# Exponentials of attention: some tiles by a polynomial on VectorE and GpSimd, the wide activations in parts

## The chip, the cores and the metric

The kernel runs on one core of a Trainium2 chip. The metric is the device time of one execution in microseconds (us), as the median of several runs. A NeuronCore has five engines, each with its own queue of instructions, which they work off in order: TensorE (PE in the profile; its weight loads are PEld), VectorE (DVE), ScalarE (ACT), GpSimd (POOL) and SyncE (SP, which here only issues transfers). They share a memory SBUF of 128 partitions; TensorE writes into PSUM, from where VectorE and ScalarE read. Engines wait for each other by semaphores.

## The reference

The network has four layers on x of 2048 positions and 640 channels: a state-space convolution, attention, the same convolution, the same attention, each behind a layer norm and added to x. The change lies in the attention, which runs twice (layers b and d in the kernel's names):

```python
x = x + _A_ref(_layernorm(x), ...)          # long convolution
x = x + _B_ref(_layernorm(x), ...)          # attention
...
q = (x @ wq).reshape(B, S, H, Dh)           # S = 2048, H = 32 heads, Dh = 20
k = x @ wk                                  # one key and one value
v = x @ wv                                  # for all heads
scores = einsum("bhqd,bkd->bhqk", q, k) * (Dh ** -0.5)
p = softmax(scores, axis=-1)
o = einsum("bhqk,bkd->bhqd", p, v)
... reshape(B, S, H * Dh) @ wo
```

Per attention layer this is 32 x 2048 x 2048, or 134 million, exponentials.

## The kernel before

One layer's scores are cut into 1024 tiles of 128 keys by 1024 columns; the columns are four heads by 256 queries. The list `tiles` runs over four blocks of 512 queries (`nb`), eight groups of four heads (`hg`), two halves of the block (`f`) and sixteen key tiles (`t`). 32 consecutive tiles belong to one head group and add up into one PSUM tile `po`.

A tile goes through three steps. `scores` (L1298) makes two matmuls into a PSUM tile `sc` of 1024 columns. The exponential is taken in one of two ways. `direct` (L1304): ScalarE reads `sc` and writes the exponentials to an SBUF tile `pt`. `aside` (L1311): VectorE copies `sc` to one half of a wide SBUF tile `pw`, and ScalarE later takes the exponentials of the 2048 columns of two such tiles in place, with one activation (L1429). `values` (L1321) multiplies the exponentials by the values, four matmuls of 256 columns, one for each head, into `po`. The value matrix has a column of ones, so that the sum of the exponentials, the softmax's denominator, comes with it.

PSUM has room for three tiles `sc` (tag `s2`, three buffers taken in turn), and two smaller banks, one for `po`, the other for the projections of the head group before. `qp`, the queries of a head group, comes by 16 transfers issued on SyncE, with three buffers; `load_q` is called when the first tile of a group is scored.

Within the loop the order of instructions on TensorE, ScalarE and VectorE is the order in which the code is written (`manual_schedule`). The loop takes six tiles per cycle: four direct, two aside. The cycle starts with the wide activation, and then has two halves. A half issues three scores, each followed by its exponential or copy (direct, aside, direct, in the order of the three PSUM buffers), then one step of a waiting list `pieces`, and then `behind`: the values of three earlier tiles, and, where a credit of 0.52 per half has reached 1, one projection (`product`, L1393) with the addition to x that follows it on VectorE (`add`, L1380).

When a head group's 32 tiles are through, `normalize` copies `po` out of PSUM (L1347) and transposes it at once; the reciprocal with a second transposition and the multiplication by it (L1352) are the two `pieces` of the next halves. The last one also issues the transfers of the result to `ot` on SyncE (L1358), from which the projections read.

Of the kernel before, what the change touches and what calls it, by code (L numbers as in the profile page):

```python
# [36 lines left out]
LIMIT = 32.0 * 20.0**0.5  # L37
SAFE = ((LIMIT - 1e-6) / 1.002) ** 2


# [155 lines left out]
class Net:  # L196
    def __init__(self, tc, ins):
        self.tc = tc
        self.nc = tc.nc
        self.ins = ins  # L200
        self.wfs = []
        self.bank = 0

    def setup(self, ctx):
# [16 lines left out]

    def ps2(self, name):
        return self.ps.tile([P, 1024], F32, tag="s2", bufs=3, name=name)

# [1037 lines left out]
    def main_loop(self, ap, mp, kt, vt, nm, out):  # L1262
# [24 lines left out]
        tiles = [(nb, hg, f, t) for nb in range(4) for hg in range(8) for f in range(2) for t in range(16)]  # L1287
        pos, pts, ots, wide = {}, {}, {}, {}
        queue, later = [], []

        def scores(i):
            nb, hg, f, t = tiles[i]
            if (nb, hg) not in qps:
                self.load_q(ap, nm, nb, hg)
            sc = self.ps2(f"sc{nm}{i}")
            for par in range(2):
                rows = slice(64 * par, 64 * par + 62)
                nc.tensor.matmul(sc[:, 512 * par : 512 * par + 512], kt[rows, 128 * t : 128 * t + 128],  # L1298
                                 qps[nb, hg][rows, f].rearrange("p a c -> p (a c)"), start=True, stop=True)
            return sc  # L1300

        def direct(i, sc):
            pts[i] = mp.tile([P, 1024], F32, tag="pt", bufs=5, name=f"pt{i}")
            nc.scalar.activation(pts[i], sc, AF.Exp, scale=SCALE)  # L1304

        def aside(i, sc):

            if i // 6 not in wide:
                wide[i // 6] = mp.tile([P, 2, 1024], F32, tag="pw", bufs=3, name=f"pw{i // 6}")
            pts[i] = wide[i // 6][:, i % 6]  # L1310
            nc.vector.tensor_copy(pts[i], sc)  # L1311

        def values(i):
            nb, hg, f, t = tiles[i]
            if (nb, hg) not in pos:
                pos[nb, hg] = self.ps1(f"po{nm}{nb}{hg}", hg % 2)
            po, pt = pos[nb, hg], pts.pop(i)

            for j in range(4):
                c0 = 512 * (j % 2) + 256 * (j // 2)  # L1320
                nc.tensor.matmul(po[32 * j : 32 * j + 32, 256 * f : 256 * f + 256], vt[:, t],  # L1321
                                 pt[:, c0 : c0 + 256], start=(t == 0), stop=(t == 15))

# [17 lines left out]
        def flat(a):  # L1341
            return a.rearrange("p a b -> p (a b)")

        def normalize(nb, hg):
            po = pos.pop((nb, hg))
            on = mp.tile([P, 512], F32, tag="on", bufs=2, name=f"on{nb}{hg}")
            nc.vector.tensor_copy(on, po)  # L1347
            inv, steps = inverses(on, f"{nb}{hg}")
            steps[0]()

            def finish():
# [8 lines left out]
                for k in range(80 * hg // 128, 80 * (hg + 1) // 128):  # L1360
                    later.extend((nb, k, u) for u in range(8))

            pieces.extend([steps[1], finish])

# [37 lines left out]

        n = len(tiles)
        credit, pieces = [0.0], []

        def behind(group):

            for i in group:
                values(i)
                if i % 32 == 31 and i + 1 < n:  # L1410
                    normalize(*tiles[i][:2])
            if not group:
                return
            if group[-1] % 32 >= (15 if group[-1] < n - 32 else 8):
                queue.extend(later)
                later.clear()
            credit[0] = min(credit[0] + 0.52, 1.5)
            if queue and credit[0] >= 1 and group[-1] % 32 not in (0, 1):
                credit[0] -= 1
                projection(tiles[group[-1]][1])  # L1420

        with tc.manual_schedule(engines={mybir.EngineType.PE, mybir.EngineType.Activation,
                                         mybir.EngineType.DVE}):
            for i, put in ((0, direct), (6, aside), (1, direct)):
                put(i, scores(i))
            for c in range(0, n, 6):
                w = wide.pop(c // 6, None)
                if w is not None:
                    nc.scalar.activation(flat(w), flat(w), AF.Exp, scale=SCALE)  # L1429
                for h in range(2):  # L1430
                    burst = [(c + 2 + 2 * h, direct), (c + 7 + 5 * h, aside), (c + 3 + 2 * h, direct)]
                    for i, put in burst:
                        if i < n:
                            put(i, scores(i))
                    if pieces:
                        pieces.pop(0)()
                    if c == 36 and h == 0:
                        late_loads(pts[38])
                    behind([i for i in range(c - 3 + 3 * h, c + 3 * h) if 0 <= i < n])
            behind([n - 1])  # L1440
            on = normalize_last()
# [8 lines left out]
            last.append(self.ps1(f"pl{nm}7", 1)[:, 0:320])  # L1450
            left = queue + later
            for u in range(8):
# [92 lines left out]
```

## Time and profile before

| what | us |
|---|---|
| median of three runs (2980.04 to 2980.66) | 2980.32 |
| the profiled execution | 2978.3 |
| its span, first to last instruction | 2976.4 |
| loop of layer b, first to last start of a direct activation | 719.7 to 1664.6 |
| loop of layer d, likewise | 2015.0 to 2958.5 |
| ScalarE busy in the span | 2414.1 |
| TensorE busy in the span | 2733.0 |
| VectorE busy in the span | 2027.1 |
| GpSimd busy in the span | 84.9 |

The profile is of one execution. A row of groups reads: line of the code, engine, operation, output<-input with their shapes, count, then busy time, mean duration of one in ns, and the engine's idle time just before them with what ended it. A row of the timeline reads: start, duration, engine, line, operation, and the count of like instructions merged into the row. Tiles of layer b end in b, those of layer d in d.

A row's duration can reach past the start of the next row on its engine: the wide activation at 1021.62 us lasts 1.91 us, and the next activation starts at 1023.43, 1.81 us later. What an instruction costs on a busy ScalarE is therefore read from start to start.

### The profile page before, as it was taken

The numbers are of one execution on the slowest core, as the hardware profiler recorded it, in microseconds if no ns is written. First come the engines' busy times: TensorE is split into PE (matmuls) and PEld (weight loads), VectorE is DVE, ScalarE is ACT, GpSimd is POOL, SyncE is SP. The second block draws the span as 40 slices with busy tenths as digits, with TensorE's granted clock in tenths as the row PEclk, the third lists the DMA queues.
The fourth block names the chain that finished last, engine by engine and source line by source line (L and its number), as shares of the span: only waits on it lengthen the run. The fifth ranks groups of instructions, "written<-read, shape, count | busy, mean of one in ns | idle before, by whom it ended". The sixth has DMA issues, their size and how long they took to land. (4 is left out here: it accounts for less than half of the span.)

```text
span 2976.4 us, 69802 instructions
## 1 busy us (share of the span) xinstructions
PE 2733.0 (92%) x29940; PEld 1570.6 (53%) x29940; DVE 2027.1 (68%) x2486; ACT 2414.1 (81%) x2565; POOL 84.9 (3%) x140
## 2 busy tenths in 40 slices
PE   2776989898999999999999998998999999999999
PEld 0333978775444444444444687774444444444444
DVE  7999899943566666666666699725566656666655
ACT  5888243454999999999999734338999999999997
POOL 0000001100000000000000011000000000000000
PEclk9655999998999999999999999999999999999999
DMA  6114555533200010101010256231001101110100
GB/s 146 34 17 103 183 167 114 139 104 104 82 23 27 22 26 22 28 21 28 23 27 20 88 114 161 65 128 43 22 27 31 35 23 32 35 28 23 44 20 24
DMA packets 144184, 178.81 MB, mean 60 GB/s; under 512 B 59524, under 2 KB 115844, under 8 KB 140244
## 3 DMA queue, kind: packets, MB, share of 16 engines
q1 hardware_dynamic: 119704, 141.90, 16.2%
q0 software_dynamic: 21872, 30.69, 5.6%
q8 instruction: 239, 3.92, 0.6%
q10 hardware_dynamic: 2288, 1.64, 0.2%
q14 instruction: 81, 0.66, 0.1%
HBM read 95.22 MB, written 48.04 MB: 48 GB/s over the span
## 5 line engine op out<-in xcount | busy, mean ns | idle before, releaser
L1304 ACT ACTIVATE pt<-scb 128x1024 f32<-128x1024 f32 x684 | 653.5, 1046 | 14.3 <-PE scb L1298 7.2
L1304 ACT ACTIVATE pt<-scd 128x1024 f32<-128x1024 f32 x684 | 652.5, 1044 | 12.7 <-PE scd L1298 7.2
L1429 ACT ACTIVATE pw<-pw 128x2048 f32<-128x2048 f32 x340 | 657.3, 1933 | 0.0
L1311 DVE COPY pw<-scd 128x1024 f32<-128x1024 f32 x340 | 415.4, 1222 | 218.1 <-PE scd L1298 215.0
L1311 DVE COPY pw<-scb 128x1024 f32<-128x1024 f32 x340 | 414.8, 1220 | 212.4 <-PE scb L1298 206.9
L1298 PE MATMUL scb<-qpb,kt 62*128 62x512 f32 x2048 | 378.6, 449 | 27.1 <-ACT pt L1304 17.7
L1298 PE MATMUL scd<-qpd,kt 62*128 62x512 f32 x2048 | 379.5, 449 | 24.4 <-ACT pt L1304 15.7
L1321 PE MATMUL pob<-pt,vt 128*32 128x256 f32 x5472 | 363.4, 383 | 0.1
L1321 PE MATMUL pod<-pt,vt 128*32 128x256 f32 x5472 | 362.9, 383 | 0.1
L1298 PEld LDWEIGHTS scb<-qpb,kt 62*128 62x128 f32 x2048 | 170.4, 186 | 260.9 <-ACT pt L1304 163.7
L1298 PEld LDWEIGHTS scd<-qpd,kt 62*128 62x128 f32 x2048 | 170.0, 185 | 259.7 <-ACT pt L1304 163.8
L1321 PEld LDWEIGHTS pob<-pt,vt 128*32 128x32 f32 x5472 | 160.6, 110 | 152.0 <-issue 63.9
L1321 PEld LDWEIGHTS pod<-pt,vt 128*32 128x32 f32 x5472 | 160.5, 110 | 152.0 <-issue 63.9
L1321 PE MATMUL pod<-pw,vt 128*32 128x256 f32 x2720 | 182.0, 385 | 1.0 <-DVE x L1380 1.0
L1321 PE MATMUL pob<-pw,vt 128*32 128x256 f32 x2720 | 182.0, 385 | 1.0 <-DVE x L1380 1.0
L1380 DVE TENSOR_TENSOR x<-pyd,x 128x320 f32<-128x320 f32 x149 | 72.6, 487 | 144.0 <-PE pyd L1393 144.0
L1380 DVE TENSOR_TENSOR x<-pyb,x 128x320 f32<-128x320 f32 x149 | 72.7, 488 | 141.0 <-PE pyb L1393 141.0
L1321 PEld LDWEIGHTS pob<-pw,vt 128*32 128x32 f32 x2720 | 71.1, 109 | 74.1 <-issue 42.4
L1321 PEld LDWEIGHTS pod<-pw,vt 128*32 128x32 f32 x2720 | 71.1, 109 | 73.3 <-issue 41.6
L1393 PE MATMUL pyb<-wo,ot 128*32 128x320 f32 x1192 | 107.5, 432 | 0.5 <-DMA ot<-on 0.5
L1393 PE MATMUL pyd<-wo,ot 128*32 128x320 f32 x1192 | 107.5, 432 | 0.4 <-DMA ot<-on 0.4
L654 PE MATMUL zc<-xnc,wf 128*128 128x256 f32 x384 | 87.4, 391 | 4.6 <-ACT xnc L821 4.5
(378 smaller groups left out, 3559.4 us busy)
## 6 DMA issues: line engine op xcount, KB each, us to landing
Akh<-kh SPq DMA_DIRECT2D x10, 2048.0 KB
kh<-Ak SPq DMA_DIRECT2D x5, 2048.0 KB
qhd<-qh SPq DMA_DIRECT2D x40, 256.0 KB
qld<-ql SPq DMA_DIRECT2D x40, 256.0 KB
qpb<-qhd SPq DMA_DIRECT2D x256, 40.0 KB
qpd<-qhd SPq DMA_DIRECT2D x256, 40.0 KB
ot<-on SPq DMA_DIRECT2D x216, 40.0 KB
wi<-in_c_wi SPq DMA_DIRECT2D x16, 512.0 KB
```

What stands on the lines that cost most here:

```text
L654: nc.tensor.matmul(zv[:, :, c, kk], self.wf[:, t + 4 * h, j, c, kk], x, start=(n == 0), stop=(n == 3))
L1298: nc.tensor.matmul(sc[:, 512 * par : 512 * par + 512], kt[rows, 128 * t : 128 * t + 128], qps[nb, hg][rows, f].rearrange("p a c -> p (a c) ...
L1304: nc.scalar.activation(pts[i], sc, AF.Exp, scale=SCALE)
L1311: nc.vector.tensor_copy(pts[i], sc)
L1321: nc.tensor.matmul(po[32 * j : 32 * j + 32, 256 * f : 256 * f + 256], vt[:, t], pt[:, c0 : c0 + 256], start=(t == 0), stop=(t == 15))
L1380: nc.vector.tensor_tensor(xh, py, xh, ALU.add)
L1393: nc.tensor.matmul(py[j : j + m], o[:, 128 * i + j : 128 * i + j + m], w[:, c0 : c0 + n], start=start, stop=stop)
L1429: nc.scalar.activation(flat(w), flat(w), AF.Exp, scale=SCALE)
```

## The change

Four things change in `main_loop`, and one in how PSUM is given out.

Every fourth cycle from the ninth on, the first of the two aside tiles becomes a polynomial tile (`powers`): 41 of some 340 aside tiles per layer. It is scored and taken out of PSUM four cycles early (`ahead`). `power` works out the exponential as a power of two. VectorE clamps and scales the scores out of PSUM into integers z, whose upper bits are the exponent and whose lower 23 bits the fraction. One further operation makes the fraction's number m, between 1 and 2, one the exponent's number e. Two operations on 512 columns each start the polynomial in m, in h (named zh in the profile), and GpSimd does the rest: four times a multiplication and addition of constants, followed by a multiplication by m, or by e at the end. z, m and e have one buffer each, h has two. The steps wait in `pieces` and are taken one per half, as those of `normalize` are.

The wide activation is taken in two parts per cycle, one ahead of each half (`exponentials`), counted in quarters of 256 columns: seven quarters per cycle from the ninth on, four in the first part and three in the second, eight before. An activation ends where a wide tile ends, so that a part can be two of them.

The copy of `po` out of PSUM becomes a piece too, put at the head of the list, and its transposition another; no projection is issued while a `po` is unread. A projection's column becomes ready two halves after its transfers are issued, by a count of halves and no longer by the place in the head group. The four matmuls of `values` go through the columns of a tile in ascending order. Each of the three PSUM tiles for scores gets its own tag; in the loop the first direct one, the aside one and the second direct one use the same three in turn as before. GpSimd's order is now that of the code, too.

```diff
-    def ps2(self, name):
-        return self.ps.tile([P, 1024], F32, tag="s2", bufs=3, name=name)
+    def ps2(self, name, k=None):
+
+        if k is None:
+            k = self.pair
+            self.pair = (k + 1) % 3
+        return self.ps.tile([P, 1024], F32, tag=f"s2{k}", bufs=1, name=name)
...
+        def exponentials(q0, q1):
+
+            while q0 < q1:
+                e = min(q1, (q0 // 8 + 1) * 8)
+                cols = asides[q0 // 8][:, 256 * (q0 % 8) : 256 * (q0 % 8) + 256 * (e - q0)]
+                nc.scalar.activation(cols, cols, AF.Exp, scale=SCALE)
+                q0 = e
+
+        def power(i, sc):
+
+            z, m, e = (mp.tile([P, 1024], I32, tag=t, bufs=1, name=f"{t}{i}") for t in ("z", "zm", "ze"))
+            h = mp.tile([P, 1024], F32, tag="zh", bufs=2, name=f"zh{i}")
+            pts[i] = blocks(h)
+            c = POW2
+            mf, ef = m.bitcast(F32), e.bitcast(F32)
+            nc.vector.tensor_scalar(z, sc, LOWEST, LOG2, ALU.max, ALU.mult)
+
+            def first(a):
+                nc.vector.scalar_tensor_tensor(h[:, a : a + 512], mf[:, a : a + 512], c[4] / c[5],
+                                               mf[:, a : a + 512], op0=ALU.add, op1=ALU.mult)
+
+            def others():
+                first(512)
+                for a, b, f in ((0.5 * c[5], 0.5 * c[3], mf), (1.0, 0.5 * c[2], mf),
+                                (1.0, 0.5 * c[1], mf), (1.0, 0.5 * c[0], ef)):
+                    nc.gpsimd.tensor_scalar(h, h, a, b, ALU.mult, ALU.add)
+                    nc.gpsimd.tensor_tensor(h, h, f, ALU.mult)
+
+            pieces.extend([
+                lambda: nc.vector.tensor_scalar(m, z, 0x7FFFFF, 0x3F800000, ALU.bitwise_and, ALU.bitwise_or),
+                lambda: first(0), others])
+            pieces.insert(len(pieces) - 2, lambda: nc.vector.tensor_scalar(
+                e, z, 0x7F800000, 0x40000000, ALU.bitwise_and, ALU.bitwise_xor))
...
-            nc.vector.tensor_copy(on, po)
             inv, steps = inverses(on, f"{nb}{hg}")
-            steps[0]()
+            unread.append(po)
+
+            def read():
+                nc.vector.tensor_copy(on, unread.pop())
...
-            pieces.extend([steps[1], finish])
+            pieces.insert(0, read)
+            pieces.extend(steps + [finish])
...
+        places = [6 * (k // 2) + 1 + k % 2 for k in range(2 * cycles)]
+        powers = {places[2 * c] for c in range(8, cycles - 2, 4)}
...
-            for c in range(0, n, 6):
-                w = wide.pop(c // 6, None)
-                if w is not None:
-                    nc.scalar.activation(flat(w), flat(w), AF.Exp, scale=SCALE)
+            for c in range(cycles):
+                want = 4 * sum(aside_of[i] >= 0 for i in aside_of if i <= places[2 * c + 1])
+                left = max(want - done, 7 if 8 <= c < cycles - 3 else 0)
                 for h in range(2):
+                    part = (left + 1) // 2 if h == 0 else left // 2
+                    if part:
+                        exponentials(done, done + part)
+                        done += part
```

How this moves the instructions is shown at three places in the middle of layer b's loop. On ScalarE before, pt and scb with a number are a direct tile and its scores, pw a wide tile; a cycle and the start of the next read:

```order
L1429 ACTIVATE pw20_11900<-pw20_11900 128x2048
L1304 ACTIVATE pt122_11983<-scb122_11980 128x1024
L1304 ACTIVATE pt123_11992<-scb123_11989 128x1024
L1304 ACTIVATE pt124_12015<-scb124_12012 128x1024
L1304 ACTIVATE pt125_12042<-scb125_12039 128x1024
L1429 ACTIVATE pw21_11960<-pw21_11960 128x2048
```

And now, on ScalarE, for the same kind of place:

```order
L1342 ACTIVATE pw14_11737<-pw14_11737 128x768
L1319 ACTIVATE pt100_11841<-scb100_11838 128x1024
L1319 ACTIVATE pt101_11850<-scb101_11847 128x1024
L1342 ACTIVATE pw14_11737<-pw14_11737 128x256
L1342 ACTIVATE pw15_11806<-pw15_11806 128x768
L1319 ACTIVATE pt102_11877<-scb102_11874 128x1024
L1319 ACTIVATE pt105_11887<-scb105_11884 128x1024
L1342 ACTIVATE pw15_11806<-pw15_11806 128x768
```

The 2048 columns ahead of four direct tiles have become 768 or 1024 columns ahead of each two, in one activation or, where a wide tile ends, in two. In the two layers together there are 880 activations of pw in place of 340.

On VectorE before, near the tiles 378 to 391 (on, tr and rc belong to `normalize`, x and pyb to a projection's addition; in brackets the engines or transfer queues that an instruction waits for):

```order
L1311 COPY pw63_14727<-scb379_14758 128x1024 [waits PE_49]
L1311 COPY pw64_14804<-scb384_14801 128x1024 [waits PE_49,Activation_49]
L1380 TENSOR_TENSOR x_66<-pyb107_14823,x_66 128x320 [waits PE_49]
L1311 COPY pw64_14804<-scb385_14835 128x1024 [waits PE_49]
L1311 COPY pw65_14864<-scb390_14861 128x1024 [waits PE_49,Activation_49]
L1311 COPY pw65_14864<-scb391_14889 128x1024 [waits PE_49]
```

And now, with the steps of the polynomial tile 409 (z, zm and ze its integers, zh its result):

```order
L1352 TENSOR_SCALAR z409_15138<-scb409_15135 128x1024 [waits PE_49]
L1366 TENSOR_SCALAR zm409_15139<-z409_15138 128x1024 [waits DVE_49,Pool_49]
L1334 COPY pw56_15170<-scb386_15167 128x1024 [waits PE_49,Activation_49]
L1368 TENSOR_SCALAR ze409_15140<-z409_15138 128x1024 [waits Pool_49]
L1440 TENSOR_TENSOR x_66<-pyb107_15190,x_66 128x320 [waits PE_49]
L1334 COPY pw56_15170<-scb391_15202 128x1024 [waits PE_49]
L1355 SCALAR_TENSOR_TENSOR zh409_15141<-zm409_15139 128x512 [waits DVE_49]
L1334 COPY pw57_15233<-scb392_15230 128x1024 [waits PE_49,Activation_49]
L1355 SCALAR_TENSOR_TENSOR zh409_15141<-zm409_15139 128x512
```

Tile 409 is taken out of PSUM ahead of tile 386. Between the copies of the halves that follow stand its steps; zm and ze wait for GpSimd, which must have read the buffers of the polynomial tile before.

On GpSimd the loop had no arithmetic before. Now each polynomial tile has these eight rows there:

```order
L1362 TENSOR_SCALAR zh409_15141<-zh409_15141 128x1024 [waits DVE_49,PE_49]
L1363 TENSOR_TENSOR zh409_15141<-zh409_15141,zm409_15139 128x1024 [waits Pool_49]
L1362 TENSOR_SCALAR zh409_15141<-zh409_15141 128x1024 [waits Pool_49]
L1363 TENSOR_TENSOR zh409_15141<-zh409_15141,zm409_15139 128x1024 [waits Pool_49]
L1362 TENSOR_SCALAR zh409_15141<-zh409_15141 128x1024 [waits Pool_49]
L1363 TENSOR_TENSOR zh409_15141<-zh409_15141,zm409_15139 128x1024 [waits Pool_49]
L1362 TENSOR_SCALAR zh409_15141<-zh409_15141 128x1024 [waits Pool_49]
L1363 TENSOR_TENSOR zh409_15141<-zh409_15141,ze409_15140 128x1024 [waits Pool_49]
```

Each waits for the one before; the last writes the exponentials that `values` reads.

More of the change, by code (lines that the diff above doesn't have):

```diff
@@ L1300, in scores, with blocks @@
             return sc
[L1302 to L1311, printed above, removed]
+        def blocks(a):
+            return [a[:, c0 : c0 + 256] for c0 in (0, 512, 256, 768)]
@@ new lines, in direct, with aside @@
+        def direct(i, k):
+            sc = scores(i, k)
+            pt = mp.tile([P, 1024], F32, tag="pt", bufs=5, name=f"pt{i}")
+            nc.scalar.activation(pt, sc, AF.Exp, scale=SCALE)
+            pts[i] = blocks(pt)
+        asides = {}
+        def aside(i, k):
+            sc = scores(i, k)
+            if i in powers:
+                power(i, sc)
+                return
+            a = aside_of[i]
+            if a // 2 not in asides:
+                asides[a // 2] = mp.tile([P, 2048], F32, tag="pw", bufs=3, name=f"pw{a // 2}")
+            cols = asides[a // 2][:, 1024 * (a % 2) : 1024 * (a % 2) + 1024]
+            nc.vector.tensor_copy(cols, sc)
+            pts[i] = blocks(cols)
@@ L1401, in projection @@
             add(nb, u, py, k == 4)
-        n = len(tiles)
-        credit, pieces = [0.0], []
+        credit, bursts = [0.0], [0]
         def behind(group):
@@ L1441, in main_loop @@
+            behind(range(6 * cycles - 3, n))
+            while pieces:
+                pieces.pop(0)()
             on = normalize_last()
```

68 lines of the change are left out of this document (42 added, 26 removed).

## The prediction

> **What bounds the kernel now.** I read the page's engine row, then the busy time in a stretch inside each attention loop, then the first and last start of the loop's activations.
>
> ```profile
> PE 2733.0 (92%) x29940; PEld 1570.6 (53%) x29940; DVE 2027.1 (68%) x2486; ACT 2414.1 (81%) x2565; POOL 84.9 (3%) x140
> ```
> ```profile
> 800.00:1600.00 800.00, 785.68 (x9786) 374.32 (x9780) 503.70 (x596) 795.73 (x726) 0.54 (x1) 1.00 0.09 25
> ```
> ```profile
> L1304 ACT ACTIVATE pt<-scb x684: 1013/1026/1202, 719.7 to 1664.6; 128x1024 f32<-128x1024 f32 x171
> ```
>
> The columns of the stretch are PE, PEld, DVE, ACT and POOL. Inside the loop ScalarE is busy for 795.73 of 800 us, VectorE for 503.70 (63%) and GpSimd for nothing. So ScalarE sets the pace there, although the whole span gives it only 81%. The loop of layer b lasts 1664.6 - 719.7 = 944.9 us; layer d's is alike, so the two are 63% of the span. A full cycle has six tiles, four direct activations and one wide one: 1024 / 6 = 170.7 cycles of 5.53 us on average.
>
> How short could a cycle be? ScalarE's timeline in layer b:
>
> ```profile
> 1021.62 1.91 ACT L1429 ACTIVATE pw<-pw 128x2048 f32<-128x2048 f32 x1
> 1023.43 3.77 ACT L1304 ACTIVATE pt<-scb 128x1024 f32<-128x1024 f32 x4
> 1027.04 1.95 ACT L1429 ACTIVATE pw<-pw 128x2048 f32<-128x2048 f32 x1
> 1028.84 3.81 ACT L1304 ACTIVATE pt<-scb 128x1024 f32<-128x1024 f32 x4
> 1032.45 1.99 ACT L1429 ACTIVATE pw<-pw 128x2048 f32<-128x2048 f32 x1
> ...
> 1054.45 1.91 ACT L1429 ACTIVATE pw<-pw 128x2048 f32<-128x2048 f32 x1
> 1056.25 3.81 ACT L1304 ACTIVATE pt<-scb 128x1024 f32<-128x1024 f32 x4
> 1059.94 1.92 ACT L1429 ACTIVATE pw<-pw 128x2048 f32<-128x2048 f32 x1
> ```
>
> From 1027.04 to 1032.45 ScalarE goes back to back: 5.41 us, of which the wide activation holds it for 1.80 and each direct one for 3.61 / 4 = 0.90. From 1054.45 to 1059.94 the same work takes 5.49. Over the loop 944.9 - 170.7 x 5.41 = 21 us per layer are lost to such small gaps. TensorE shows where they come from:
>
> ```profile
> 1060.64 0.97 PE L1298 MATMUL scb<-qpb,kt 62*128 62x512 f32 x6
> 1061.54 1.50 PE L1321 MATMUL pob<-pt,vt 128*32 128x256 f32 x24
> 1062.97 1.26 PE L1298 MATMUL scb<-qpb,kt 62*128 62x512 f32 x6
> 1064.17 1.07 PE L1321 MATMUL pob<-pw,vt 128*32 128x256 f32 x16
> 1065.06 0.61 PE L1321 MATMUL pob<-pt,vt 128*32 128x256 f32 x8
> 1065.49 0.72 PE L1393 MATMUL pyb<-wo,ot 128*32 128x320 f32 x8
> 1066.14 0.97 PE L1298 MATMUL scb<-qpb,kt 62*128 62x512 f32 x6
> ```
>
> A half cycle on TensorE is three score tiles (0.90 from start to start), three tiles of values (1.43) and sometimes a projection (0.65). The second scores of the cycle take 1.20: the third tile waits for ScalarE to free its PSUM buffer, because the wide activation of 1.8 us ran just ahead of the direct ones. TensorE needs 2 x 2.33 + 0.65 = 5.31 in a cycle with one projection, and 5.31 + 0.30 passes 5.41. So the two engines are coupled: ScalarE's halves last 3.6 and 1.8 us, TensorE's 2.3 to 3.0.
>
> **ScalarE: what is taken off, what is added.** Per layer 41 tiles of 1024 columns leave ScalarE, and the 170 wide activations become 440 shorter ones (ScalarE's order has 880 rows of them in the two layers, and 340 before), 270 more. The price of a column and of an instruction comes from activations whose input and output lie in SBUF, by their starts:
>
> ```profile
> 142.47 1.06 ACT L435 ACTIVATE fa<-f 128x1024 f32<-128x1024 f32 x1
> 143.43 1.04 ACT L436 ACTIVATE s<-f 128x1024 f32<-128x1024 f32 x1
> 144.38 1.13 ACT L437 ACTIVATE c<-fa,halfpi 128x1024 f32<-128x1024 f32 x1
> ```
>
> 1024 columns hold ScalarE for 0.95 to 0.96 us, 2048 for 1.80 to 1.81: 0.85 per 1024 columns and 0.10 per instruction. Taken off: 41 x 0.85 = 34.9. Added: 270 x 0.10 = 27. Net 7.9 us per layer, 16 in both; with the ends of the rounding (0.12 and 0.84, or 0.09 and 0.86) it is 4 to 22. Per cycle that is 5.36 instead of 5.41. By itself the polynomial buys little: the splitting eats three quarters of it.
>
> **The gaps.** With two parts per cycle ScalarE's half is about 0.9 + 1.8 = 2.7 us both times, beside TensorE's 2.33 or 2.98. TensorE may then start its scores anywhere from 0.3 to 1.4 us after the first buffer comes free without anybody waiting; before, the second half left 0.45. Of the 21 us about 5 are at the loop's start, where nothing changes:
>
> ```profile
> ACT pt L1304 <- PE scb L1298: 7.2, 15, 2.2
> ACT pt L1304 <- PE pob L1321: 1.3, 1, 1.3
> PEld scb L1298 <- ACT pt L1304: 163.2, 365, 0.8
> PEld scb L1298 <- DVE pw L1311: 13.8, 31, 1.2
> ```
>
> Three columns: total, times, longest. The longest waits (2.2 and 1.3) are the start's. The other 16 per layer, 32 in both, I count as regained; the late copy of po, one cause of the waits on DVE (31, one per head group), moves behind the next tile's copy too. TensorE's average need, 4.66 + 0.86 x 0.65 = 5.2 per cycle (147 projections in 171 cycles), stays under 5.36, but by 3% only: it is next in line.
>
> **VectorE.** A polynomial tile's first step out of PSUM replaces its copy at the same price. Added per tile: two operations on 1024 integers and two on 512 columns with two inputs.
>
> ```profile
> L1311 DVE COPY pw<-scb 128x1024 f32<-128x1024 f32 x340 | 414.8, 1220 | 212.4 <-PE scb L1298 206.9 <-ACT pt L1304 1.2
> L1380 DVE TENSOR_TENSOR x<-pyb,x 128x320 f32<-128x320 f32 x147 | 71.7, 488 | 134.6 <-PE pyb L1393 134.6
> L1352 DVE TENSOR_TENSOR on<-on,tr 128x512 f32<-128x512 f32 x31 | 21.1, 682 | 0.0
> ...
> L232 DVE TENSOR_SCALAR r<-ph 128x1024 bf16<-128x1024 f32 x40 | 48.8, 1219 | 7.9 <-PE ph L412 7.6 <-DMA hdare<-hare 0.3
> L117 DVE SCALAR_TENSOR_TENSOR Aa<-B 128x512 f32<-128x512 f32 x36 | 22.6, 687 | 0.3
> ...
> L278 DVE TENSOR_SCALAR th<-rA_A_im,dt 128x128 f32<-128x128 f32 x5 | 1.1, 283 | 4.8 <-DMA rA_A_im<-in_A_A_im 4.8
> L232 DVE TENSOR_SCALAR frac<-th 128x640 f32<-128x640 f32 x2 | 1.0, 490 | 0.0
> ```
>
> From PSUM a scalar operation (1219) costs what the copy does (1220). In SBUF 128 to 640 columns add 207 ns, so 1024 take about 0.65; whether integers run so fast no row shows, so the upper end is 1.22. With 2 x 0.69 a tile adds 2.7 to 3.8 us, every eighth half: 0.33 to 0.48 per half on top of 0.63 x 2.77 = 1.74, in all 2.1 to 2.2 of 2.68. So it fits, hidden behind ScalarE, with about 0.5 us to spare per half. Without that cover, each half in which a copy comes over 1 us late would hold the next score tile and then ScalarE. Queued behind each of these pieces are the copies of the next halves and the adds of the projections.
>
> **GpSimd.** Each tile has four scalar and four two-input operations of 1024 columns, each waiting for the one before. No row of before shows such an operation; the nearest are its fills:
>
> ```profile
> L1280 POOL MEMSET wol<- 128x640 f32 x2 | 1.3, 636 | 233.9 <-PEq L1249 233.9
> L1329 POOL MEMSET ot<- 128x512 f32 x2 | 1.1, 542 | 499.6 <-DMA ot<-on 499.6
> ```
>
> One pass over 1024 columns is about 0.94 us by these. If an operation takes one pass, a tile takes 7.5 us; if it takes a pass for every tensor it reads or writes (two and three), 18.8. I take 14, a little over the middle, for the waits between the eight. The Trainium skill (GPSIMD Engine Reference, section "Performance versus the Vector engine") measures a two-input addition of 2048 columns at 4497 ns on GpSimd, so as an estimate 2.25 for 1024; with the fills for the rest a tile takes about 13 and the term below for the hold falls to nothing, 2932 in all. No run here shows it yet.
>
> What 14 us must fit into follows from the loop: the last piece of a tile stands 6 halves ahead of its values for one tile in four, 8 to 10 for the others. Six halves less the 0.8 between the places inside them are 15.3 us: no wait of TensorE. A closer limit is the single buffer of the exponent part: for one tile in four, VectorE's step ze comes 4.8 halves = 12.9 us after GpSimd began the tile before it, and must wait until that tile is done: 14 - 12.9 = 1.1 us. Half of it I let through VectorE's spare time to ScalarE: 0.55 x 20.5 groups of four in both layers = 11 us. GpSimd's own load, 14 of 21.4 us, is otherwise beside the path; its DMA issues (wol, wf, out) wait behind it and nothing waits for them.
>
> **SyncE.** A polynomial tile is scored four cycles early, and with it the loads of its head group's queries move up, each group's 16 of them on SP:
>
> ```profile
> 1014.45 0.66 SPq L1078 DMA_DIRECT2D qpb<-qhd  x2
> ...
> 1020.08 0.26 SPq L1088 DMA_DIRECT2D qpb<-mxd  x1
> ```
>
> They take 5.9 us to issue. Their buffer comes free when the group three before has been scored, by the loop 11 to 17 halves (29 us or more) before the first score that needs them, and the transfers of ot that stand ahead of them on SP are done by then. I cost this at nothing; with half that distance it would still be covered.
>
> **The sum.** -16 - 32 + 11 = -37 us, against the profiled execution's 2978.3 (span 2976.4), which lies 2 us under the median of 2980.3: 2943 as a median.
>
> **Rivals.** *The polynomial comes too late* (GpSimd slower than 16 us per tile). For: no row shows its operations, and the single buffers chain tiles together. Against: the fills. At 17 us the tile with 6 halves is 1.7 late for TensorE, and ze is held 4.1, of which half counts: 3.75 x 20.5 = 77, less the 48 gained: +29, 3009. It decides from 16 us, where 0.7 + 1.6 = 2.3 per group eat the 48. At 18.8 it is 3.5 + 3.0, so 133 - 48 = +85.
>
> *VectorE becomes the bound, held up by GpSimd.* If an operation of VectorE that reads two SBUF tensors, or takes two columns at a time, cannot run beside GpSimd, then per eight halves 4.75 operations (four of the tile's and 0.75 of on<-on,tr) each lose half a GpSimd instruction. At 1.75 us an instruction and GpSimd busy 65% this is 4.75 x 0.88 x 0.65 / 8 = 0.34 per half, 2.5 of 2.68: still hidden. At 2.7 us and 88% it is 0.7, 2.8 to 2.9 per half against today's 2.77: with 2.83, 341 x 2 x 0.06 = +41, 3021. Deciding point: 0.5 us per half. The Trainium skill (SBUF — State Buffer, section "Who interferes with whom") says that the shared port pair is an exclusive lock and the second to issue blocks fully. The trace of before has nothing running on GpSimd beside VectorE, so no row speaks for or against it.
>
> *No change:* the splitting costs 0.12 (4 us gained), a quarter of the gaps comes back (8), and the hold takes 11: 2979. For it: TensorE's margin of 3%.
>
> **The numbers.** Forecast 0.62, for itself 2918 to 2965 (everything regained, 22 + 42 with the start's; or half of the gaps, -16 - 16 + 11). No change 0.10. Late polynomial 0.20, held VectorE 0.08. About 0.2%, 6 us, is what a measurement of this kernel can tell from no change. So faster 0.62, same 0.10, slower 0.28. The range runs from 2918 to 3015: it leaves out the ends of the two slow cases, where most of these lie beyond 17 us or the full hold.
>
> **What would show it.** Right: a ScalarE cycle of about 5.36, 880 activations of pw, GpSimd's pairs at 3.5 us together, few waits of TensorE for zh. Wrong: values that wait for GpSimd, ze with holds of over 3 us, copies on VectorE that begin over 1 us after their scores, or two-input steps of 512 columns far over 0.69 us.

## The result and the profile after

The changed kernel takes 3117.87 us (median of four runs, 3116.16 to 3121.19) against 2980.49 for the kernel before on the same chip: a ratio of 1.046, 95% interval 1.0443 to 1.0479. That is 137 us slower, where 2943 was forecast and the range ended at 3015. The profiled execution has a span of 3116.5 us against 2976.4.

The engine row of the page, one stretch inside layer b's loop (columns PE, PEld, DVE, ACT, POOL, then TensorE's clock), and the first and last start of the direct activations:

```profile
PE 2756.6 (88%) x29928; PEld 1576.6 (51%) x29928; DVE 2272.6 (73%) x2812; ACT 2399.3 (77%) x3105; POOL 1247.6 (40%) x796
```
```profile
800.00:1600.00 800.00, 739.36 (x9108) 350.98 (x9106) 573.80 (x696) 733.90 (x894) 480.92 (x272) 0.97 0.09 23
```
```profile
L1319 ACT ACTIVATE pt<-scb x684: 1015/1075/1357, 722.1 to 1734.3; 128x1024 f32<-128x1024 f32 x171
L1319 ACT ACTIVATE pt<-scd x684: 1014/1085/1382, 2086.3 to 3096.4; 128x1024 f32<-128x1024 f32 x171
```

Layer b's loop now lasts 1012.2 us, 67 more than its 944.9 before, and layer d's 1010.1; the two loops hold nearly all of the 140 us by which the spans differ. In the stretch ScalarE is idle for 66 of 800 us where it was idle for 4, and no other engine has become full: VectorE is at 72%, GpSimd at 60%. TensorE's clock, 0.97 instead of 1.00 in the stretch, is not what costs the time: one of the four runs had 0.962 over the whole span and took 3116.16 us, the others 0.935 to 0.939 and 3117.25 to 3121.19. So something waits in turn. The waits (total, times, longest) say what:

```profile
DVE zm L1366 <- POOL zh L1363: 155.0, 40, 6.3
...
DVE ze L1368 <- POOL zh L1363: 85.9, 40, 2.3
ACT pt L1319 <- PE scd L1309: 85.7, 53, 5.5
...
ACT pt L1319 <- PE scb L1309: 82.7, 57, 5.5
...
PE scb L1309 <- DVE pw L1334: 42.6, 23, 4.8
```

VectorE stands still for 241 us in front of zm and ze until GpSimd has read the tile before; TensorE then lacks a copy, and ScalarE lacks scores. One such event on the timeline of layer b, from GpSimd's start to ScalarE (in brackets the idle time ahead of an instruction and what ended it):

```profile
1069.54 1.06 POOL L1362 TENSOR_SCALAR zh<-zh 128x1024 f32<-128x1024 f32 x1 [15.66 <-DVE zh L1355]
...
1072.79 1.23 DVE L1352 TENSOR_SCALAR z<-scb 128x1024 int32<-128x1024 f32 x1 [0.17 <-PE scb L1309]
...
1077.91 2.34 POOL L1363 TENSOR_TENSOR zh<-zh,zm 128x1024 f32<-128x1024 f32 x1
1080.28 0.69 DVE L1366 TENSOR_SCALAR zm<-z 128x1024 int32<-128x1024 int32 x1 [6.27 <-POOL zh L1363]
...
1080.89 1.22 DVE L1334 COPY pw<-scb 128x1024 f32<-128x1024 f32 x1
...
1082.16 1.22 PE L1309 MATMUL scb<-qpb,kt 62*128 62x512 f32 x4 [4.79 <-DVE pw L1334]
...
1083.49 1.02 ACT L1319 ACTIVATE pt<-scb 128x1024 f32<-128x1024 f32 x1 [4.11 <-PE scb L1309]
...
1084.36 0.69 DVE L1368 TENSOR_SCALAR ze<-z 128x1024 int32<-128x1024 int32 x1 [2.25 <-POOL zh L1363]
```

GpSimd begins a tile at 1069.54. The next tile's z follows only 3.25 us later, its zm is next in VectorE's queue at 1074.0 (1080.28 less the wait of 6.27), and zm may overwrite its one buffer only after the sixth of GpSimd's eight operations, at 1080.25. The copy behind it starts 6 us late, and 4.1 us of that reach ScalarE. A half later ze waits for the eighth operation.

The costs themselves, in the groups (count, busy time, mean ns):

```profile
L1363 POOL TENSOR_TENSOR zh<-zh,zm 128x1024 f32<-128x1024 f32 x246 | 588.1, 2391 | 20.5
L1362 POOL TENSOR_SCALAR zh<-zh 128x1024 f32<-128x1024 f32 x328 | 377.2, 1150 | 998.6 <-DVE zh L1355 524.1 <-ACT pt L1319 294.4 <-PE scd L1309 85.1
...
L1366 DVE TENSOR_SCALAR zm<-z 128x1024 int32<-128x1024 int32 x82 | 93.3, 1138 | 157.2 <-POOL zh L1363 155.0
...
L1411 DVE TENSOR_TENSOR on<-on,tr 128x512 f32<-128x512 f32 x62 | 63.3, 1021 | 0.0
...
L1368 DVE TENSOR_SCALAR ze<-z 128x1024 int32<-128x1024 int32 x82 | 56.3, 687 | 85.9 <-POOL zh L1363 85.9
```

A tile on GpSimd is 4 x 1.15 + 4 x 2.39 = 14.2 us. Two rows of VectorE are longer than they need be without any wait being named: zm with a mean of 1138 ns, where a single one takes 0.69 us, and on<-on,tr with 1021 ns where it took 682 before. Taken one by one, the 40 zm that waited for GpSimd lasted 0.69 us; of the 42 others 22 lasted 0.69 and 20 lasted 1.94 to 2.70, and each of these 20 ended 0.5 to 0.6 us after an operation of GpSimd.

### The profile page after: what moved, and what is told of

It is laid out like the page before. It is cut to its first block, busy times and chain, and to the rows that moved or that the text cites. A ratio compares the mean times of both kernels' runs of the same rounds, so it can differ in the third digit from the quotient of the medians.

```text
span 3116.5 us, 71537 instructions
## 1 busy us (share of the span) xinstructions
PE 2756.6 (88%) x29928; PEld 1576.6 (51%) x29928; DVE 2272.6 (73%) x2812; ACT 2399.3 (77%) x3105; POOL 1247.6 (40%) x796
## 5 line engine op out<-in xcount | busy, mean ns | idle before, releaser
L1362 POOL TENSOR_SCALAR zh<-zh 128x1024 f32<-128x1024 f32 x328 | 377.2, 1150 | 998.6 <-DVE zh L1355 524.1
L1319 ACT ACTIVATE pt<-scd 128x1024 f32<-128x1024 f32 x684 | 688.7, 1095 | 88.1 <-PE scd L1309 85.7
L1319 ACT ACTIVATE pt<-scb 128x1024 f32<-128x1024 f32 x684 | 686.7, 1088 | 90.1 <-PE scb L1309 82.7
L1342 ACT ACTIVATE pw<-pw 128x768 f32<-128x768 f32 (+3 forms) x880 | 718.1, 859 | 0.0
L1363 POOL TENSOR_TENSOR zh<-zh,zm 128x1024 f32<-128x1024 f32 x246 | 588.1, 2391 | 20.5
L1334 DVE COPY pw<-scd 128x1024 f32<-128x1024 f32 x299 | 365.5, 1222 | 104.6 <-PE scd L1309 90.3
L1334 DVE COPY pw<-scb 128x1024 f32<-128x1024 f32 x299 | 364.9, 1220 | 101.1 <-PE scb L1309 92.8
L1366 DVE TENSOR_SCALAR zm<-z 128x1024 int32<-128x1024 int32 x82 | 93.3, 1138 | 157.2 <-POOL zh L1363 155.0
L1363 POOL TENSOR_TENSOR zh<-zh,ze 128x1024 f32<-128x1024 f32 x82 | 195.6, 2385 | 6.8
L1368 DVE TENSOR_SCALAR ze<-z 128x1024 int32<-128x1024 int32 x82 | 56.3, 687 | 85.9 <-POOL zh L1363 85.9
```

What stands on the lines that cost most here:

```text
L1319: nc.scalar.activation(pt, sc, AF.Exp, scale=SCALE)
L1334: nc.vector.tensor_copy(cols, sc)
L1342: nc.scalar.activation(cols, cols, AF.Exp, scale=SCALE)
L1362: nc.gpsimd.tensor_scalar(h, h, a, b, ALU.mult, ALU.add)
L1363: nc.gpsimd.tensor_tensor(h, h, f, ALU.mult)
L1366: lambda: nc.vector.tensor_scalar(m, z, 0x7FFFFF, 0x3F800000, ALU.bitwise_and, ALU.bitwise_or),
```

## The experiments

The first theory: VectorE's queue is held at the single buffers of zm and ze (the hold, below). The rivals: GpSimd slows VectorE's operations in SBUF (rival 1), or the two parts and the new order of the work cost the time (rival 2). Ratios are against the kernel before, with 95% intervals; loop lengths are first to last start of the direct activations, as above.

**e1: two buffers for zm and ze, in layer d.** Layer b, where no memory is left for them, is the control.

```diff
-z, m, e = (mp.tile([P, 1024], I32, tag=t, bufs=1, ...) for t in ("z", "zm", "ze"))
+z, m, e = (mp.tile([P, 1024], I32, tag=t, bufs=b, ...) for t, b in
+           (("z", 1), ("zm", 2 if out is not None else 1), ("ze", 2 if out is not None else 1)))
```

> zm and ze get a second buffer in layer d only (layer b has no memory left for it), so layer b of the same run is the control: its loop stays at 1012 us. Theory (VectorE's queue held at the single buffers of zm and ze): d's loop falls from 1010 to 920 to 945, the whole to 3028 to 3053, and the idle time of VectorE at zm and ze behind GpSimd, 241 us in all, falls to about 120, all of it in layer b. Rival 1 (GpSimd's work slows VectorE's operations through what they share in SBUF): d's loop stays over 990, since GpSimd runs as much as before. Rival 2 (the parts and the new order themselves cost): d's loop stays over 990 as well, with ScalarE waiting for TensorE where TensorE waits for no copy.

Measured: 3066.37 us, 1.0290 (1.0273 to 1.0307). Layer b stays at 1013, layer d falls from 1010 to 961: between theory and rivals. The groups of layer d's loop:

```profile
L1367 DVE TENSOR_SCALAR zm<-z 128x1024 int32<-128x1024 int32 x41 | 73.9, 1802 | 3.2
L1356 DVE SCALAR_TENSOR_TENSOR zh<-zm 128x512 f32<-128x512 f32 x82 | 65.2, 796 | 0.0
L1369 DVE TENSOR_SCALAR ze<-z 128x1024 int32<-128x1024 int32 x41 | 63.3, 1544 | 0.0
...
L1412 DVE TENSOR_TENSOR on<-on,tr 128x512 f32<-128x512 f32 x31 | 33.2, 1070 | 0.0
```

The waits for a buffer are gone, but zm and ze now take 1.80 and 1.54 us, 2.0 us per tile more than 0.69 each. In the changed kernel's layer d, VectorE waited 121 us for the buffers, zm took 1.14, ze 0.69 and a step of 512 columns 0.68. So 121 us of waits are gone and 73 us have come back as longer rows, and the difference of 48 is what the loop gained, 49. Both the hold and rival 1 are at work; the 49 us are what is left after both, not the price of the hold alone.

**e2: two buffers for zm only.** The edit is that of e1 without ze.

> Only zm gets a second buffer, in layer d only. In the changed kernel half of the tiles wait at zm (3.9 us each) and then at ze (2.1 more). Theory: the wait moves to ze, which needs the last of GpSimd's eight operations where zm needs the sixth, so that nearly all of it remains: d's loop 1000 to 1010, VectorE's waits at zm in layer d gone, those at ze about 120 us there instead of 43. If the two waits were costs that add up, d's loop would fall by about 45, to 965. Rival (shared SBUF access): no change, and the waits at ze stay at 2 us each.

Measured: 3133.04 us, 1.0513 (1.0495 to 1.0530), with layer d at 1025.9: slower than the changed kernel. VectorE's wait in layer d:

```profile
DVE ze L1369 <- POOL zh L1364: 95.3, 20, 7.9
```

The two waits are one: what zm no longer waits for, ze does, up to 7.9 us at a time. The loop became even longer than expected (1000 to 1010). zm takes 1.57 us in layer d instead of 1.14, but the waits there fell from 121 to 95 us, so that VectorE loses 8 us less than in the changed kernel; why the loop is 16 us longer all the same is not shown.

**e3: no polynomial, only the parts and the order.**

```diff
-powers = {places[2 * c] for c in range(8, cycles - 2, 4)}
+powers = set()
...
-left = max(want - done, 7 if 8 <= c < cycles - 3 else 0)
+left = max(want - done, 8 if 8 <= c < cycles - 3 else 0)
```

> No tile by the polynomial at all, so that only the two parts per cycle and the new order of copies remain; four blocks of 256 columns in each half. By the prediction's terms ScalarE pays 170 more instructions of 0.10 us per layer (+17) and gets 16 us of gaps back: 945 us per loop, 2980 in all, within 15. Rival 2 (the parts and the new order cost the 137 us): 3050 or more. If the gaps come back without the price of an instruction: 2950.

Measured: 2996.01 us, 1.0055 (1.0038 to 1.0072), just past the end of the 15 us allowed. Rival 2 is dead as the cause of 137 us, but the parts by themselves lose 16. ScalarE's timeline, one cycle from 1062.54 to 1068.05:

```profile
1062.54 1.29 ACT L1342 ACTIVATE pw<-pw 128x1024 f32<-128x1024 f32 x1
1063.49 2.18 ACT L1319 ACTIVATE pt<-scb 128x1024 f32<-128x1024 f32 x2
1065.29 1.31 ACT L1342 ACTIVATE pw<-pw 128x1024 f32<-128x1024 f32 x1
1066.24 2.19 ACT L1319 ACTIVATE pt<-scb 128x1024 f32<-128x1024 f32 x2
1068.05 1.33 ACT L1342 ACTIVATE pw<-pw 128x1024 f32<-128x1024 f32 x1
```

5.51 us without a gap, 0.10 more than the 5.41 of before: the price of one more activation, as the prediction had it. The rows name 5 us per layer in which ScalarE waits for scores, at the loop's start.

**e4: the polynomial's pieces ahead of normalize's.** Buffers stay single; in layer b GpSimd starts a tile every 20 to 26 us instead of every 20 to 33.

```diff
-pieces.extend([m, first(0), others])          # then ze ahead of the last two
+at = len(unread)
+pieces[at:at] = [m, ze, first(0), others]
```

> The buffers stay single, but the four pieces of a polynomial tile go ahead of normalize's transposes instead of behind them, so that GpSimd begins a tile every 7 to 9 halves instead of 6 to 11, and the next tile's zm stands 4 halves (about 10.7 us) or more behind GpSimd's start instead of 2. Theory: zm needs the sixth operation, 10.7 us after the start, so the waits fall from 241 us to under 40 in all, and the time to 2930 to 2965. Rival 1 (shared SBUF access): 3050 or more, since every operation is still there. Rival 2 (the parts): the same 3050.

Measured: 2999.57 us, 1.0072 (1.0055 to 1.0089): 118 us of the changed kernel's loss are gone by an order alone, but not the 150 to 190 expected. What VectorE still waits for:

```profile
DVE ze L1369 <- POOL zh L1363: 45.4, 23, 2.3
DVE zm L1367 <- POOL zh L1363: 30.0, 20, 1.7
```

75 us instead of the 40 expected, and zm, with a mean of 1.69 us in layer b, is slowed as in e1.

**e5: GpSimd does two of its eight operations.** The other six are left out, so the polynomial is incomplete; all other engines do what they did in the changed kernel.

```diff
-for a, b, f in ((0.5 * c[5], 0.5 * c[3], mf), (1.0, 0.5 * c[2], mf), (1.0, 0.5 * c[1], mf), (1.0, 0.5 * c[0], ef)):
+for a, b, f in ((0.5 * c[5], 0.5 * c[3], ef),):
```

> The changed kernel with only the first and the last of GpSimd's eight operations per tile (one scalar, one two-input, about 3.5 us instead of 14.4); the other six are left out, so the polynomial is not the reference's. VectorE, ScalarE and TensorE do all that they did. Theory (the hold at zm and ze, and beside it GpSimd's operations that keep VectorE's zm, ze and two-input steps from starting, seen in layer d of the run with doubled buffers as zm 1.88 and ze 1.57 us where 0.69 are enough): both go, so the loops fall to 920 to 932 and the whole to 2930 to 2955. Rival (TensorE, 3 per cent under ScalarE, or the parts themselves hold the loop): 945 or more per loop as in the runs with the polynomial ahead or with doubled buffers, 2980 or more in all.

Measured: 2948.47 us, 0.9895 (0.9879 to 0.9912), loops of 928.5 and 926.6, as the theory said. Layer b's stretch and two groups of VectorE in layer d:

```profile
800.00:1600.00 800.00, 792.38 (x9980) 378.54 (x9973) 605.89 (x758) 799.54 (x982) 129.33 (x75) 1.00 0.09 25
```
```profile
L1365 DVE TENSOR_SCALAR zm<-z 128x1024 int32<-128x1024 int32 x33 | 22.8, 691 | 0.9
...
L1410 DVE TENSOR_TENSOR on<-on,tr 128x512 f32<-128x512 f32 x24 | 16.4, 681 | 0.0
```

ScalarE is busy for 799.54 of 800 us, zm takes 0.69 and on<-on,tr 0.68 again. So what six of GpSimd's eight operations cost, by the places where they stand, is 3117.87 - 2948.47 = 169 us; without them the change gains 31.

**e6: fixed halves.** zm stands one half behind z, ze and the first 512 columns two, the rest with GpSimd's start three. With a tile every eight halves, GpSimd should then have been done for up to 2 us when zm comes.

```diff
-pieces.extend([...])
+for wait, call in ((1, m), (2, ze), (2, first(0)), (3, others)):
+    due.setdefault(half[0] + wait, []).append(call)
...
+for call in due.pop(half[0], []):             # in each half, ahead of pieces
+    call()
+half[0] += 1
```

> All eight operations and single buffers, but the pieces of a polynomial tile stand at fixed halves after its z: zm one later, ze and the first 512 columns two, the rest and GpSimd's start three. A tile begins every 8 halves (21.4 us), GpSimd is busy for 14.4 of them, so zm and ze come when it has been idle for 0 to 2 us. Theory: no waits at zm and ze (under 20 us in all), both at 0.69 us, loops of 922 to 938, 2935 to 2965 in all, so faster than before. If only the hold counted and not the slowed operations: as with the polynomial ahead less its 75 us of waits. Rival (the parts or TensorE): 2985 or more.

Measured: 2971.64 us, 0.9973 (0.9962 to 0.9984): just faster than before, 7 us above the range expected; loops of 942.1 and 936.3. VectorE in layer d's loop:

```profile
L1366 DVE TENSOR_SCALAR zm<-z 128x1024 int32<-128x1024 int32 x41 | 28.4, 692 | 0.0
L1411 DVE TENSOR_TENSOR on<-on,tr 128x512 f32<-128x512 f32 x31 | 28.2, 909 | 0.0
L1367 DVE TENSOR_SCALAR ze<-z 128x1024 int32<-128x1024 int32 x41 | 27.9, 681 | 0.0
```

No waits, and 0.69 and 0.68 us for zm and ze; on<-on,tr, which was not moved, still takes 0.91 instead of 0.68. That is full GpSimd work, single buffers, and 146 us less than the changed kernel, by places alone.

**e7: the same in one part per cycle.**

```diff
-part = (left + 1) // 2 if h == 0 else left // 2
+part = left if h == 0 else 0
```

> The same fixed halves, but the seven blocks of a cycle go through ScalarE in one burst at its start instead of two: about 1.75 instructions per cycle instead of 2.6, which at 0.10 to 0.13 us saves 15 to 19 us per loop, while the gaps of before (16 to 21 us per loop) may come back because ScalarE's halves are uneven again. Theory: within 15 us of the run with two parts, so 2930 to 2975. If the halving is what brings the gain: 2975 to 3000.

Measured: 2995.66 us, 1.0057 (1.0040 to 1.0074). That is 24 us more than e6, so the halving is needed. ScalarE in the half without a part, and TensorE's scores late for it:

```profile
1061.34 1.94 ACT L1319 ACTIVATE pt<-scb 128x1024 f32<-128x1024 f32 x2 [0.93 <-PE scb L1309]
```

**e8: GpSimd's start two halves later, two buffers in layer d.** No buffer can be waited for in layer d, but zm, ze and, as it was expected, the first 512 columns fall into GpSimd's busy time. This tells rival 1 from the hold.

```diff
-(2, first(0)), (3, others)
+(2, first(0)), (5, others)                    # and the buffers of e1
```

> The kernel with fixed halves, with one thing moved: the last 512 columns and with them GpSimd's start stand five halves behind z instead of three, and layer d has two buffers for zm and ze. In d nothing waits for a buffer, but the next tile's zm, ze and first 512 columns now fall into the 14.4 us in which GpSimd is busy. Theory (VectorE's fast one-input steps and its two-input steps cannot run beside a GpSimd operation and wait for its end): zm and ze go from 0.69 to 1.5 to 1.9 us each and the 512-column step from 0.68 to about 1.2, with no wait named; d's loop from 936 to 950 to 965. If only waiting for buffers costs: d's loop stays at 936. Layer b, with single buffers, waits at zm or ze for about 1 us a tile on top.

Measured: 3179.99 us, 1.0667 (1.0651 to 1.0683); layer d's loop goes from 936.3 to 1034.2, far over the 950 to 965 expected, with no wait for GpSimd named. (Layer b, with single buffers, goes from 942 to 1055; there zm and ze wait 117 us in all, 2.9 per tile where about 1 was expected.) VectorE and GpSimd in layer d:

```profile
2316.19 2.39 POOL L1364 TENSOR_TENSOR zh<-zh,zm 128x1024 f32<-128x1024 f32 x1
...
2317.17 1.96 DVE L1367 TENSOR_SCALAR zm<-z 128x1024 int32<-128x1024 int32 x1
...
2318.67 1.37 POOL L1363 TENSOR_SCALAR zh<-zh 128x1024 f32<-128x1024 f32 x1
2319.05 0.48 DVE L1441 TENSOR_TENSOR x<-pyd,x 128x320 f32<-128x320 f32 x1
...
2319.45 1.21 DVE L1334 COPY pw<-scd 128x1024 f32<-128x1024 f32 x1
...
2320.13 2.39 POOL L1364 TENSOR_TENSOR zh<-zh,ze 128x1024 f32<-128x1024 f32 x1
...
2320.58 2.48 DVE L1368 TENSOR_SCALAR ze<-z 128x1024 int32<-128x1024 int32 x1
```

zm begins beside a GpSimd operation that ends at 2318.58 and is done 0.55 us after it; ze ends at 2323.06, 0.54 after the next one's 2322.52. Of the 82 zm and ze of layer d, 77 end 0.5 to 0.6 us after an operation of GpSimd. GpSimd's operation behind zm takes 1.37 instead of 1.05. The copy out of PSUM and the addition with one input in PSUM keep their 1.21 and 0.48. So by these rows VectorE's zm and ze and GpSimd's operations run one at a time, and the profile shows it as a longer instruction (the lock, below). The Trainium skill (SBUF — State Buffer, section "Who interferes with whom") calls the shared port pair an exclusive lock, held for the whole instruction, with the second to come blocked fully; these rows agree. The groups of layer d's loop:

```profile
L1368 DVE TENSOR_SCALAR ze<-z 128x1024 int32<-128x1024 int32 x41 | 100.4, 2449 | 0.0
...
L1367 DVE TENSOR_SCALAR zm<-z 128x1024 int32<-128x1024 int32 x41 | 75.1, 1831 | 0.0
```

So VectorE loses (1.83 + 2.45 - 1.38) x 41 = 119 us in layer d, and the loop grows by 98. The expectation was too low because it put ze at 1.5 to 1.9 and let only part of that through. The steps of 512 columns, expected at 1.2, kept their 0.68: they stand behind ze, which ends only when GpSimd is done.

**e9: parts that end with a buffer.** ScalarE's parts are chosen so that none reaches past the end of a wide tile and none needs two activations: 340 of them instead of 440 per layer, for the same columns.

```diff
+if 8 <= c < cycles - 3:
+    lag = first + 3.5 * (2 * c + h - 15) - done
+    part = {0: 4 if lag > 1.5 else 3, 3: 3, 4: 4, 6: 2}[done % 8]
```

> Fixed halves, and ScalarE's parts chosen so that none crosses the end of a buffer of eight blocks (4 and 4, or 3, 3 and 2): 340 instructions on pw per layer instead of 440, the same columns. At 0.10 to 0.13 us an instruction 10 to 13 us per loop: 924 to 932 for b, 922 to 927 for d, 2945 to 2952 in all. If the halves with only 2 blocks leave TensorE behind (up to 0.5 us in 40 halves per layer), half of it is lost: 2952 to 2962. If the price of an instruction were nothing, since TensorE is the next limit: 2972.

Measured: 2965.33 us, 0.9949 (0.9936 to 0.9963), 6 us under e6 where 20 to 27 were expected. The uneven halves are not what eats it, since e10 keeps them; TensorE waits elsewhere (layer b's row; layer d's has 14.9 us):

```profile
PE pyb L1453 <- DVE on L1408: 15.4, 15, 1.6
```

The projection waits for the copy of po, which the fixed pieces had pushed back in its half. e6 has nearly as much of this wait, 12.3 and 11.5 us; e10 tries whether it is what limits both.

**e10: the copy of po first, and no projection in its half.**

```diff
+fresh[0] = bool(unread)
+if pieces: pieces.pop(0)()                    # ahead of the due calls now
 for call in due.pop(half[0], []): call()
...
-if queue and credit[0] >= 1 and not unread and group:
+if queue and credit[0] >= 1 and not unread and not fresh[0] and group:
```

> The kernel with fixed halves and aligned parts; the copy of po goes ahead of the polynomial's pieces in its half instead of behind them, and no projection stands in that half. Theory: what is left of waiting, TensorE's projection for that copy (13 us in 700, 12 times) and ScalarE behind it (9.4), goes: 10 us less per loop, 2945 to 2958 in all. If these waits are covered, or the next late thing takes their place: 2963 to 2968, as without the edit.

Measured: 2939.19 us, 0.9862 (0.9845 to 0.9880), 6 us below the range expected; it beats both kernels, with all of GpSimd's work. The order of the copy and the place of the projection were changed together, so the 26 us against e9 belong to the two. Layer b's stretch and ScalarE's waits in the whole run:

```profile
800.00:1600.00 800.00, 793.66 (x10040) 384.94 (x10036) 608.19 (x759) 796.75 (x895) 520.53 (x299) 1.00 0.09 25
```
```profile
ACT pt L1319 <- PE scb L1309: 14.3, 19, 4.6
...
ACT pt L1319 <- PE scd L1309: 7.7, 13, 2.3
```

ScalarE is idle for 3 of 800 us, and waits 22 us for scores in all instead of 168. The loops last 923.4 and 921.7 us.

## Why the prediction was wrong, point by point

**ScalarE's price: right.** An activation more costs 0.10 us (e3). Two cycles of the changed kernel that nothing disturbs, by the starts of the same part one cycle apart (the row x2 merges one of 256 and one of 768 columns):

```profile
1055.99 0.86 ACT L1342 ACTIVATE pw<-pw 128x768 f32<-128x768 f32 x1
...
1058.53 1.10 ACT L1342 ACTIVATE pw<-pw 128x1024 f32<-128x1024 f32 x1
...
1061.29 0.90 ACT L1342 ACTIVATE pw<-pw 128x768 f32<-128x768 f32 x1
...
1063.83 1.22 ACT L1342 ACTIVATE pw<-pw 128x256 f32<-128x256 f32 x2
...
1066.68 0.94 ACT L1342 ACTIVATE pw<-pw 128x768 f32<-128x768 f32 x1
```

With two activations of pw a cycle takes 5.30 us, with three 5.39. At 440 activations in 171 cycles the mean is the 5.36 of the forecast.

**The gaps: half right.** They come back with one part (e7). But in e5, where GpSimd works little, the loops last 928.5 and 926.6 us, where the forecast's two terms for ScalarE leave 921.0 and 919.6. These 14.5 us are most of the 16 by which e5 (2948) missed the 2932 that the sum gives without its hold. The undisturbed cycles of e5 take 5.30 and 5.39 us as well, so the rest are single halves that are some tenths longer. The profile names no wait there, because a row's duration can reach past the next start: in e5 the part of 768 columns at 1055.46 us holds ScalarE for 1.04 us, the one at 1050.13 for 0.73. So of the 32 us that were counted as regained, about 17 came back; e3 says the same, with 10 and 9 of the 16 per layer. In the half named, TensorE had done a projection in each of two halves running and began its scores late; what lengthens the others is open.

**GpSimd's tile: right, in part by luck.** 14.2 us against 14, which was picked a little over the middle of 7.5 to 18.8 with no row to support it. The operation with constants came out near one pass over the columns (1.05 us undisturbed), the two-input operation at 2.39. The estimate of 2.25 from the Trainium skill (GPSIMD Engine Reference, section "Performance versus the Vector engine") was near it.

**VectorE's operations: right by themselves.** z out of PSUM 1.22; zm, ze and the halves of 512 columns 0.68 to 0.69 where GpSimd is idle, near the lower bound of 0.65.

**The hold: the step that failed.** The prediction says: "A closer limit is the single buffer of the exponent part: for one tile in four, VectorE's step ze comes 4.8 halves = 12.9 us after GpSimd began the tile before it", and takes 1.1 us, half of it, 20.5 times: 11 us. The mechanism was the right one, but three things in that step were wrong. The closest pair is another: where normalize's steps stand ahead of a tile's last piece, GpSimd starts late, and the next tile's z follows 3.25 us behind it and its zm could start 4.5 us behind it, where the step put ze at 12.9. The buffer that binds first is that of zm, which the step left out; it needs the sixth operation, and ze only takes the rest (e2). And it is half of the tiles, 40 of 82, not a quarter. The rows of waits give 155.0 + 85.9 = 241 us in place of 1.1 x 20.5 = 23, before any share is taken. With the lock, which the sum had at nothing, this term is what failed: 169 us in place of 11 (e5 against the changed kernel), 158 too few. Together with the 16 by which e5 missed its sum that is the 175 us between the forecast and the measurement.

**Half of it through to ScalarE: about right in this kernel, but no constant.** VectorE loses 241 us in waits, 37 in longer zm and 21 in longer on<-on,tr, 299 in all, and 169 of these arrive (e5). In layer d of e8 it is 98 of 119. The slack of 0.5 us per half can't cover 6 us in one half.

**The rival "VectorE held up by GpSimd": present, and given 0.08.** In the changed kernel it costs VectorE the 58 us just named, against 241 of waits. It is the smaller part because a zm that has waited for GpSimd's last use of its buffer starts just as GpSimd's operation ends: all 40 of these lasted 0.69 us, while 20 of the 42 others lasted up to 2.70. It shows in full as soon as the buffers are doubled: 2.0 us per tile in e1, 2.9 in e8. Its price of half a GpSimd instruction per operation was of the right size; what it takes from the loop was not, since the prediction hid all of it below 0.5 us per half. The prediction's remark that the trace of before has nothing of GpSimd's beside VectorE is not quite so: 36 of GpSimd's 40 fills of 0.16 us stand beside r<-ph, too short to decide anything.

**Late values, SyncE's loads: rightly at nothing.** The list of waits has none of TensorE for zh, and ScalarE's waits for the queries stay those of the loop's start.

What stays open: how much of e8's 98 us comes from zm, from ze and from their standing in neighbouring halves was not separated; how the changed kernel's 169 us divide between the hold and the lock is not shown either, since the one grows where the other is taken away (e1).

## What to carry to other kernels

When two engines hand a single buffer back and forth, work out the shortest distance from the release to the next writer over the whole order, after every other list has put its pieces between, and for each buffer by itself: the average distance says nothing, and the instruction that waits holds all that is queued behind it. More buffers help less if the two engines also shut each other out of SBUF; here a fixed place in the other engine's idle window took away both for zm and ze, and was worth 74 us in layer d's loop where doubled buffers were worth 49. After each repair look for the next late thing: the last 26 us lay in the place of a copy of 0.7 us in its half and of the projection behind it.

## What the runs showed of the hardware

A GpSimd operation on 1024 float32 columns took 1.05 us with one tensor input (two scalar operations in one) and 2.39 with two. VectorE's bitwise operations on 1024 int32 columns in SBUF took 0.69 us, against 1.22 for an operation out of PSUM. Such a step, issued while GpSimd worked, took up to 2.93 us (zm in e1) and ended 0.5 to 0.6 us after GpSimd's operation (77 of 82 in e8's layer d); its whole delay stood in the profile as busy time of VectorE, not as a wait. on<-on,tr, with two inputs in SBUF, took up to 2.48 us in the changed kernel instead of 0.68. The copy out of PSUM kept its 1.21 us beside GpSimd (e8).
